# Attention and feed-forward kernel on one core: conversions merged four slots after their first operation instead of three, raw loads a slot later, the second group normalised on ScalarE

## The chip, the cores and the metric

The kernel runs on one core of a Trainium2 chip. The time is device microseconds of one execution; several runs are taken and their median is compared. PE is TensorE (matmuls; PEld its weight loads), DVE is VectorE, ACT is ScalarE, POOL is GpSimd, SP is SyncE, which here issues all DMAs.

## What is computed

Causal attention over 4 batches, 12 heads, 448 positions and a head size of 64, then RMS normalisation and a gated feed-forward layer on all 1792 rows:

```python
attn = softmax(where(causal, q @ k.T / 8, -1e9))      # per batch and head
x    = concat_heads(attn @ v)                          # 1792 x 768
xn   = x / sqrt(mean(x * x) + 1e-6) * rms_g
g    = xn @ w_gate                                     # 768 x 1536
out  = (silu(g) * (xn @ w_val)) @ w_out                # back to 768
```

The three weight matrices come as 64-bit floats and are turned into 32-bit floats on the core. Each feed-forward product is formed from split operands (a high part and the remainder), so that it takes three matmuls.

## The kernel before

**Groups.** Attention is cut into 60 units, each one pair of heads of one batch (or two batches for the last short pieces) and a range of queries. Units 0 to 11 are the first group, 12 to 23 the second, 24 to 59 the third. While the attention of a group runs, the feed-forward part of the group before it runs between its pieces: the feed-forward of group 1 (512 rows) beside the attention of group 2, and so on. The third group's feed-forward comes at the end with no attention beside it.

**Slots.** The order of all instructions is written out by a loop on the host. It counts slots (`tick`, L137): in each slot it issues six feed-forward matmuls (`ffn_part`, L426, two of the six chunks of a weight unit, so three slots make a unit of 18 matmuls), then perhaps one step of attention, and then whatever was posted for this slot. `post(n, f)` (L131) puts `f` n slots later. The numbers n are in the table `T` (L44). Each engine executes its instructions in the order of issue, so a slot later means behind other instructions in that engine's queue.

**Weight units.** There are 36 units of weights (gate and value chunks alternate, then the output matrix). For each:

- `load_w` (L357) loads the raw 64-bit words into one of three buffers (tag `w64`), in the DMA queue of SP.
- `convert_ops` (L368) has five operations with slots c0, c1, c2, c3, c5: ACT scales the high word into the new tile `w_c` (L379); POOL clears the high words that are not wanted (L380), which waits for ACT's operation; DVE merges low and high words (L382), which waits for POOL's, and then merges them into `w_c` (L384); SP stores `w_c` to DRAM (L386) for later. L384 is the last reader of the raw buffer.
- `split_w` (L389) casts `w_c` to the high part `w_h` on ACT (L394), and DVE or POOL forms the remainder `w_l` (L396 on DVE in this stretch).

The conversion of unit s+5 begins, the split of unit s+3 is posted, in the last slot of unit s; the load of unit s+7 is posted at the beginning of unit s, `ld` slots later.

**Evictions.** A unit's 18 matmuls fill one of two PSUM banks `m`. `evict` (L446) empties it on DVE: for a gate unit into `gr` (L457), followed by a tanh on ACT (L458) and a product (L459); for a value unit into `t_sb` (L467), followed by the cast `hh` (L468, ACT) and the remainder `hl` (L470, DVE). PE can begin unit s only when unit s-2 has been evicted, since it takes the same bank.

**Attention of a unit.** Scores on PE (L192), the masked, scaled copy with its minimum on DVE (L201), the exponential on ACT (L204, and L227 for the sums), the reciprocal on DVE (L213), the normalising of the four pieces (`norms`; L207 on ACT or L209 on POOL), transposes on PE (L249), copies of these out of PSUM (L253 DVE, L255 ACT), and the products with v (L275, PE). Which engine normalises is decided in `softmax` (L195): before, ACT has it for units 15 to 23, POOL for all others. `norm` (L212) runs seven slots after the scores in this group.

Of the kernel before, what the change touches and what calls it, by code (L numbers as in the profile page):

```python
# [38 lines left out]
        for g in range(NG) for c in range(NP)}  # L39
ENDS = [max(i for i, u in enumerate(UNITS) if u[0] == g) + 1 for g in range(NG)]  # L40
MASKED = -8.0e9


T = dict(c0=0, c1=1, c2=3, c20=12, c3=3, c30=13, c26=6, c36=7, c5=5, c50=16, c56=9, exp=1, exp0=3, gt=1, hh=1, hl=4, ws=5, ld2=7,  # L44
         ld=3, ld1=11, lv=5, norm0=7, norm1=2, r0=1, r1=5, so=3, wl=2, wl0=7, wl2=5, wl4=0, xl=2, xl0=9)
LOAD = (4, 12, 24, 36, 48, 60, 74, 86)
CONVERT = (20, 32, 44, 56, 62, 93)
SPLIT = (33, 45, 57, 70)
# [14 lines left out]
def attention_ffn(ctx: ExitStack, tc: tile.TileContext, qk0, qk1, qk2, v, v2, w, g, out, out2):  # L63
# [30 lines left out]
    def bank(tag, bufs=1):  # L94


        return ps.tile([P, W], F32, tag=tag, name=tag + "_ps", bufs=bufs)

    def f32(ap):
        return ap.bitcast(F32)  # L100
# [30 lines left out]
    def post(delay, fn):  # L131
        if delay <= 0:
            fn()
        else:
            later.setdefault(now[0] + delay, []).append(fn)
# [7 lines left out]
    xr, xh, xl, acc, xq = {}, {}, {}, {}, {}  # L143
# [6 lines left out]
    def load_qk(p):  # L150
        if p < len(UNITS):
            _, kind, _, _, row, _ = UNITS[p]
            raw_qk[p] = raw.tile([P, 2, W], F32, tag="qk", name="qk_r")
            if kind == 2:
                nc.sync.dma_start(out=raw_qk[p], in_=qk2[row])
            else:
                nc.sync.dma_start(out=raw_qk[p][:, 0], in_=(qk0, qk1)[kind][row])
# [10 lines left out]
    def blocks(kind):  # L168

        return [(0, P), (P, 2 * P)] if kind == 0 else [(0, KEYS[kind])]  # L170

    def steps_s(p):


        if not 0 <= p < len(UNITS):
            return []
        _, kind, _, _, _, _ = UNITS[p]
        pr = hs[p] = dict(norms=[])
        bl = blocks(kind)
        nb = 2 * len(bl)  # L180

        def scores(pss):
            for i, (o, wd) in enumerate(bl):
                for h in range(1 + (kind == 2)):
                    for e in range(2):
                        r = raw_qk[p][e * D: (e + 1) * D, h]
                        if kind == 2:
                            ps, q0, nq = pss[e][h * D: (h + 1) * D, :wd], 0, D
                        else:
                            ps, q0, nq = pss[e][:, o: o + wd], i * P, P  # L190
                        k0 = nq if kind else 2 * P
                        nc.tensor.matmul(ps, r[:, q0: q0 + nq], r[:, k0: k0 + wd],  # L192
                                         start=True, stop=True)

        def softmax(e, i, pss):  # L195
            o, wd = bl[i]
            ps, sp = pss[e][:, o: o + wd], pr["sp"][e][:, o: o + wd]
            n = len(bl) * e + i
            nm, sm, rs = (pr[m][:, n: n + 1] for m in ("nm", "sm", "rs"))
            mk = mask2 if kind == 2 else mask[:, 3 * P - wd:]  # L200
            nc.vector.tensor_tensor_reduce(  # L201
                out=sp, in0=ps, in1=mk, scale=nsc, scalar=3.0e38,
                op0=ALU.add, op1=ALU.min, accum_out=nm)
            post(T["exp" if p >= ENDS[0] else "exp0"], lambda: nc.scalar.activation(  # L204
                sp, sp, AF.Exp, bias=nm, scale=-1.0, accum_out=sm))
            if ENDS[0] + 3 <= p < ENDS[1]:
                pr["norms"].append(lambda: nc.scalar.mul(sp, sp, rs))  # L207
            else:
                pr["norms"].append(lambda: nc.gpsimd.tensor_scalar(  # L209
                    sp, sp, rs, 1.0, op0=ALU.mult, op1=ALU.mult))  # L210

        def norm():  # L212
            nc.vector.reciprocal(pr["rs"][:, :nb], pr["sm"][:, :nb])  # L213
            for f in pr["norms"]:
                f()

        def step():
            for nm in ("nm", "sm", "rs"):
                pr[nm] = st_p.tile([P, 4], F32, tag=nm, name=nm)
            pr["sp"] = [sp_p.tile([P, S], F32, tag="sp", name="sp") for _ in range(2)]  # L220
            pss = [bank(t_) for t_ in "xy"] if p > ENDS[1] + DP and p % 2 == 0 else [
                bank("s", 2) for _ in range(2)]
            scores(pss)
            for e in range(2):
                for i in range(len(bl)):
                    softmax(e, i, pss)
            post(T["exp" if p >= ENDS[0] else "exp0"], lambda: nc.scalar.activation(  # L227
                pr["sm"][:, :nb], pr["sm"][:, :nb], AF.Identity, bias=tiny))
            post(T["norm1" if kind else "norm0"], norm)
            post(2, lambda: load_qk(p + 4))  # L230

        return [step]
# [64 lines left out]
    def square(b, c):  # L297
# [19 lines left out]
        if c == NP - 1:  # L317
            post(T["r1" if b else "r0"], lambda: rms(b, [acc[b, 0]] if b else [acc[b, 0], sq]))
        waiting.append((b, c))

    def split_x():
        if not waiting:
# [5 lines left out]
        nc.scalar.mul(h, x, gc)  # L328
        post(T["xl0" if b == 0 and c < NP - 1 else "xl"], lambda: nc.vector.scalar_tensor_tensor(
            out=l, in0=x, scalar=gc, in1=f32(h), op0=ALU.mult, op1=ALU.subtract))  # L330
        xh[b, c], xl[b, c] = h, l

    def rms(b, parts):

        ps = bank("t")
        for i, sq in enumerate(parts):
            nc.tensor.matmul(ps, ones, sq, start=(i == 0), stop=(i == len(parts) - 1))
        r = rinv[b] = rm_p.tile([P, W], F32, tag="rms", name="rms", bufs=2)
        nc.scalar.activation(r, ps, AF.Sqrt, bias=eps, scale=1.0 / DM)
        for i in range(W // P):  # L340
            sl = slice(i * P, (i + 1) * P)
            post(i if b else 1, lambda sl=sl: nc.vector.reciprocal(r[:, sl], r[:, sl]))
# [25 lines left out]
    def convert_ops(s):  # L368
# [6 lines left out]
        hf_ = raw_w.bitcast(F32)[:, :, 1]  # L375
        at2, at3, at5 = [T[n] for n in ("c20 c30 c50" if s < 5 else "c26 c36 c56" if s == 5 else "c2 c3 c5").split()]

# [427 lines left out]
    with tc.manual_schedule():  # L805
# [157 lines left out]
        for q in range(21):  # L963
            i, p = divmod(q, 3)
# [58 lines left out]
```

## Time and profile before

| | us |
|---|---|
| median of three runs | 699.96 (698.40 to 701.52) |
| the profiled execution | 699.28 |
| its span, first to last instruction | 697.5 |
| PE busy in the span | 672.7 |
| DVE, ACT, POOL busy | 534.1, 371.7, 321.5 |

The conversions run from the beginning to about 240 us. The change bears on those from unit 6 on, that is on the stretch from about 70 us on. Engine busy shares are of the whole span; PE's idle time is what the span can lose as long as PE's work stays the same. PEclk in a view is TensorE's granted clock, 1.00 being 2.4 GHz and 0.50 being 1.2 GHz.

### The profile page before, as it was taken

What the parts mean: (1) busy time and instruction counts of PE and PEld (TensorE: products, weight loads), DVE (VectorE), ACT (ScalarE), POOL (GpSimd) and SP (SyncE); (2) the same over time, 40 slices, a digit from 0 to 9 for tenths busy, and PEclk for the clock granted to TensorE, in tenths of its full rate; (3) what the DMA queues carried; (4) which work ended last, traced back from release to release, by engine and by line L of the source; (5) the groups of instructions that cost most, each with busy time, mean ns of one, the idle gap of its engine ahead of it and who ended that gap; (6) DMA issues with size and microseconds to landing.
All of it is one profiled execution on the core that took longest, in us unless ns stands there. A gap on an engine that the chain in (4) does not pass through costs nothing. (4 is left out here: it accounts for less than half of the span.)

```text
span 697.5 us, 11924 instructions
## 1 busy us (share of the span) xinstructions
PE 672.7 (96%) x4108; PEld 551.0 (79%) x4108; DVE 534.1 (77%) x1048; ACT 371.7 (53%) x832; POOL 321.5 (46%) x293
## 2 busy tenths in 40 slices
PE   9889799999999999999999999999999999999997
PEld 6456676677677777777778676888999999999997
DVE  4996988778887867677777878479386768679993
ACT  6974556876868544544545455444433433355550
POOL 4993263121223536567485756754354536312220
PEclk9999999999999999999999999999999999999999
DMA  8663878687769647667667674334657576552541
GB/s 268 225 223 108 250 220 264 201 279 209 241 203 343 219 139 207 208 223 242 203 206 229 197 237 156 123 121 133 200 184 247 180 246 207 206 159 81 168 139 68
DMA packets 71356, 138.80 MB, mean 199 GB/s; under 512 B 7744, under 2 KB 39232, under 8 KB 71296
## 3 DMA queue, kind: packets, MB, share of 16 engines
q1 hardware_dynamic: 71296, 138.05, 61.3%
q8 instruction: 32, 0.52, 0.3%
q14 instruction: 28, 0.23, 0.1%
HBM read 104.21 MB, written 33.82 MB: 198 GB/s over the span
## 5 line engine op out<-in xcount | busy, mean ns | idle before, releaser
L209 POOL TENSOR_SCALAR sp<-sp,rs 128x384 f32<-128x384 f32 (+3 forms) x132 | 95.8, 743 | 90.5 <-DVE rs L213 79.8
L440 PE MATMUL m_ps<-xh,w_h 128*128 128x512 f32 x276 | 119.0, 431 | 5.6 <-DVE gr L457 3.7
L204 ACT ACTIVATE sp<-sp,nm 128x384 f32<-128x384 f32 (+3 forms) x168 | 87.2, 522 | 43.5 <-DVE nm L201 43.5
L442 PE MATMUL m_ps<-xh,w_l 128*128 128x512 f32 x276 | 109.5, 397 | 0.0
L441 PE MATMUL m_ps<-xl,w_h 128*128 128x512 f32 x276 | 109.4, 396 | 0.0
L380 POOL TENSOR_SCALAR w<-w 128x768 f32<-128x768 f32 x36 | 36.6, 1017 | 98.1 <-ACT w_c L379 78.4
L103 POOL TENSOR_TENSOR a_l<-w_q,a_h 128x768 fp32r<-128x768 f32 x24 | 47.3, 1969 | 66.6 <-ACT a_h L481 66.5
L275 PEld LDWEIGHTS a_ps<-pt,v_r 128*64 128x64 f32 (+1 forms) x864 | 42.2, 137 | 37.5 <-DVE pt L253 10.4
L275 PE MATMUL a_ps<-pt,v_r 128*64 128x128 f32 (+2 forms) x864 | 60.8, 268 | 9.6 <-DVE pt L253 5.8
L440 PEld LDWEIGHTS m_ps<-xh,w_h 128*128 128x128 f32 x276 | 52.6, 191 | 19.2 <-issue 8.1
L103 POOL TENSOR_TENSOR w_l<-w_r,w_h 128x768 fp32r<-128x768 f32 x30 | 59.6, 1993 | 7.0 <-ACT w_h L394 6.9
L442 PEld LDWEIGHTS m_ps<-xh,w_l 128*128 128x128 f32 x276 | 52.5, 190 | 12.0
L253 DVE COPY pt<-t_ps 128x384 f32<-128x384 f32 (+1 forms) x71 | 42.5, 598 | 23.7 <-PE t_ps L249 23.3
L441 PEld LDWEIGHTS m_ps<-xl,w_h 128*128 128x128 f32 x276 | 52.9, 192 | 8.1 <-issue 0.2
L440 PE MATMUL m_ps<-hh,w_h 128*128 128x512 f32 x144 | 58.6, 407 | 0.0
L201 DVE CUSTOM_DVE_ANT_0 sp<-s_ps,mask 128x128 f32<-128x128 f32 (+3 forms) x136 | 49.8, 415 | 9.6 <-PE s_ps L192 8.6
L441 PE MATMUL m_ps<-hl,w_h 128*128 128x512 f32 x144 | 56.3, 391 | 0.7 <-DVE hl L470 0.7
L442 PE MATMUL m_ps<-hh,w_l 128*128 128x512 f32 x144 | 56.3, 391 | 0.0
L249 PE MATMUL t_ps<-ident,sp 128*128 128x128 f32 (+1 forms) x309 | 50.3, 275 | 0.4 <-POOL sp L209 0.2
L249 PEld LDWEIGHTS t_ps<-ident,sp 128*128 128x128 f32 (+1 forms) x309 | 38.0, 138 | 14.9 <-POOL sp L209 2.2
L382 DVE SCALAR_TENSOR_TENSOR w<-w 128x768 int32<-128x768 int32 x36 | 36.2, 1006 | 14.4 <-POOL w L380 14.4
L192 PE MATMUL s_ps<-qk_r 64*128 64x128 f32 (+3 forms) x296 | 42.2, 420 | 0.5 <-DVE nm L201 0.4
(185 smaller groups left out, 1671.1 us busy)
## 6 DMA issues: line engine op xcount, KB each, us to landing
w<-in_w SPq DMA_DIRECT2D x36, 768.0 KB, 5.1
w<-w_c SPq DMA_DIRECT2D x36, 384.0 KB, 5.7
w_r<-w SPq DMA_DIRECT2D x36, 384.0 KB, 4.9
qk_r<-in_qk SPq DMA_DIRECT2D x48, 256.0 KB, 4.4
qk_r<-in_qk SPq DMA_DIRECT2D x12, 512.0 KB, 5.6
v_r<-in_v SPq DMA_DIRECT2D x12, 448.0 KB, 5.2
v_r<-in_v SPq DMA_DIRECT2D x24, 192.0 KB, 3.0
wy<-w_r SPq DMA_DIRECT2D x24, 192.0 KB, 4.0
```

Source lines behind the costliest of these rows:

```text
L103: nc.gpsimd.tensor_tensor(out_, a, b, op=op)
L192: nc.tensor.matmul(ps, r[:, q0: q0 + nq], r[:, k0: k0 + wd], start=True, stop=True)
L201: nc.vector.tensor_tensor_reduce(out=sp, in0=ps, in1=mk, scale=nsc, scalar=3.0e38, op0=ALU.add, op1=ALU.min, accum_out=nm)
L204: post(T["exp" if p >= ENDS[0] else "exp0"], lambda: nc.scalar.activation(sp, sp, AF.Exp, bias=nm, scale=-1.0, accum_out=sm))
L209: pr["norms"].append(lambda: nc.gpsimd.tensor_scalar(sp, sp, rs, 1.0, op0=ALU.mult, op1=ALU.mult))
L249: nc.tensor.transpose(ps[:kb, at: at + P], pr["sp"][e][:, o + kb * j: o + kb * (j + 1)], ident)
L253: nc.vector.tensor_copy(pt[:kb, :at], ps[:kb, :at])
L275: nc.tensor.matmul(av_ps[e * D: (e + 1) * D, p % 2, q0: q0 + n], raw_v[p][:kb, h, j, e, :], pr["pt", e][:kb, a0: a0 + n], start=(j == 0), ...
L380: (T["c1"], lambda: nc.gpsimd.tensor_scalar(hf_, hf_, 0.0, 1.0, op0=ALU.mult, op1=ALU.mult)),
L440: nc.tensor.matmul(ps, wh[:, k, :], mh, start=(first and k == ks[0]), stop=False)
L441: nc.tensor.matmul(ps, wh[:, k, :], ml, start=False, stop=False)
L442: nc.tensor.matmul(ps, wl[:, k, :], mh, start=False, stop=(last and k == 5))
```

## The change

```diff
@@ -41,8 +41,8 @@
 MASKED = -8.0e9
 
 
-T = dict(c0=0, c1=1, c2=3, c20=12, c3=3, c30=13, c26=6, c36=7, c5=5, c50=16, c56=9, exp=1, exp0=3, gt=1, hh=1, hl=4, ws=5, ld2=7,
-         ld=3, ld1=11, lv=5, norm0=7, norm1=2, r0=1, r1=5, so=3, wl=2, wl0=7, wl2=5, wl4=0, xl=2, xl0=9)
+T = dict(c0=0, c1=1, c2=4, c20=12, c3=4, c30=13, c26=6, c36=7, c5=6, c50=16, c56=9, exp=1, exp0=3, gt=1, hh=1, hl=4, ws=5, ld2=7,
+         ld=4, ld1=11, lv=5, norm0=7, norm1=2, r0=1, r1=5, so=3, wl=2, wl0=7, wl2=5, wl4=0, xl=2, xl0=9)
 LOAD = (4, 12, 24, 36, 48, 60, 74, 86)
 CONVERT = (20, 32, 44, 56, 62, 93)
 SPLIT = (33, 45, 57, 70)
@@ -203,7 +203,7 @@
                 op0=ALU.add, op1=ALU.min, accum_out=nm)
             post(T["exp" if p >= ENDS[0] else "exp0"], lambda: nc.scalar.activation(
                 sp, sp, AF.Exp, bias=nm, scale=-1.0, accum_out=sm))
-            if ENDS[0] + 3 <= p < ENDS[1]:
+            if ENDS[0] <= p < ENDS[1]:
                 pr["norms"].append(lambda: nc.scalar.mul(sp, sp, rs))
             else:
                 pr["norms"].append(lambda: nc.gpsimd.tensor_scalar(
```

Four entries of the table and one condition are changed. Units are counted from 0. For conversions of unit 6 and later, the two merges on DVE (L382, L384) are posted four slots after the conversion's first operation, not three; the store of the converted unit (L386) six, not five; the raw load (L360) of unit 8 and later four slots after the beginning of the unit that issues it, not three. The condition in `softmax` now gives ACT the normalising of units 12 to 14 too, 12 instructions that POOL had. The number and order of PE's instructions stay as they are; DVE keeps its number of instructions.

The first place is DVE's queue around the eviction of unit 4 (`gr` from `m_ps`), for which PE waits before unit 6. (In names, `w64` is a raw buffer, `w_c` a converted unit, and the last number tells one tile from another.) Before:

```order
L384 SCALAR_TENSOR_TENSOR w_c_981<-w_c_981,w64_911 128x768
L459 SCALAR_TENSOR_TENSOR t_sb_1010<-t_sb_1010,gr_1009 128x512
L467 TENSOR_TENSOR t_sb_1010<-t_sb_1010,x_ps_986 128x512
L396 TENSOR_TENSOR w_l_1040<-w_c_961,w_h_1039 128x768
L382 SCALAR_TENSOR_TENSOR w64_964<-w64_964 128x768
L384 SCALAR_TENSOR_TENSOR w_c_1042<-w_c_1042,w64_964 128x768
L457 TENSOR_TENSOR gr_1071<-m_ps_1048,rms_924 128x512
L470 TENSOR_TENSOR hl_1037<-t_sb_1010,hh_1036 128x512
L459 SCALAR_TENSOR_TENSOR t_sb_1072<-t_sb_1072,gr_1071 128x512
L201 ISA sp_1095,nm_1092<-s_ps_1097,mask_104 128x128
```

And now:

```order
L459 SCALAR_TENSOR_TENSOR t_sb_1009<-t_sb_1009,gr_1008 128x512
L467 TENSOR_TENSOR t_sb_1009<-t_sb_1009,x_ps_984 128x512
L382 SCALAR_TENSOR_TENSOR w64_911<-w64_911 128x768
L384 SCALAR_TENSOR_TENSOR w_c_979<-w_c_979,w64_911 128x768
L396 TENSOR_TENSOR w_l_1038<-w_c_961,w_h_1037 128x768
L457 TENSOR_TENSOR gr_1069<-m_ps_1046,rms_924 128x512
L470 TENSOR_TENSOR hl_1035<-t_sb_1009,hh_1034 128x512
L382 SCALAR_TENSOR_TENSOR w64_968<-w64_968 128x768
L384 SCALAR_TENSOR_TENSOR w_c_1040<-w_c_1040,w64_968 128x768
L459 SCALAR_TENSOR_TENSOR t_sb_1070<-t_sb_1070,gr_1069 128x512
```

The pair L382, L384 stood ahead of the eviction `gr` and stands behind it and behind L470 now; the pair ahead of L396 is the one of the conversion before, which has moved in the same way, behind L467.

The second place is ACT's queue a little later, behind the first operation of a conversion (L379), where the exponentials of the next unit (L204) follow. Before:

```order
L394 CAST w_h_1075<-w_c_981 128x768
L379 ACTIVATE w_c_1078<-w64_983 128x768
L204 ACTIVATE sp_1095,sm_1093<-sp_1095,nm_1092 128x128
L204 ACTIVATE sp_1095,sm_1093<-sp_1095,nm_1092 128x256
L204 ACTIVATE sp_1096,sm_1093<-sp_1096,nm_1092 128x128
L204 ACTIVATE sp_1096,sm_1093<-sp_1096,nm_1092 128x256
L227 ACTIVATE sm_1093<-sm_1093,tiny_121 128x4
```

And now:

```order
L394 CAST w_h_1073<-w_c_979 128x768
L379 ACTIVATE w_c_1076<-w64_1006 128x768
L207 ACTIVATE sp_994<-sp_994,rs_993 128x128
L207 ACTIVATE sp_994<-sp_994,rs_993 128x256
L207 ACTIVATE sp_995<-sp_995,rs_993 128x128
L207 ACTIVATE sp_995<-sp_995,rs_993 128x256
L204 ACTIVATE sp_1093,sm_1091<-sp_1093,nm_1090 128x128
L204 ACTIVATE sp_1093,sm_1091<-sp_1093,nm_1090 128x256
L204 ACTIVATE sp_1094,sm_1091<-sp_1094,nm_1090 128x128
```

Four normalising operations of unit 12 stand between L379 and the exponentials. The same happens for units 13 and 14. They were POOL's before (L209), between two of its L380.

The third place is DVE's queue around the eviction of a value unit later in the stretch, where PE waits for `t_sb`. Before:

```order
L459 SCALAR_TENSOR_TENSOR t_sb_1987<-t_sb_1987,gr_1986 128x512
L396 TENSOR_TENSOR w_l_1997<-w_c_1878,w_h_1996 128x768
L382 SCALAR_TENSOR_TENSOR w64_1881<-w64_1881 128x768
L384 SCALAR_TENSOR_TENSOR w_c_1999<-w_c_1999,w64_1881 128x768
L467 TENSOR_TENSOR t_sb_1987<-t_sb_1987,m_ps_2006 128x512
```

And now:

```order
L459 SCALAR_TENSOR_TENSOR t_sb_1985<-t_sb_1985,gr_1984 128x512
L396 TENSOR_TENSOR w_l_1995<-w_c_1876,w_h_1994 128x768
L467 TENSOR_TENSOR t_sb_1985<-t_sb_1985,m_ps_2004 128x512
L382 SCALAR_TENSOR_TENSOR w64_1890<-w64_1890 128x768
L384 SCALAR_TENSOR_TENSOR w_c_1997<-w_c_1997,w64_1890 128x768
```

The eviction L467 has moved ahead of the pair of merges. SP's queue keeps its instructions; a raw load (L360) moves behind a load of queries and keys (L157) in some units, and ahead of none.

## Rows read from the trace of the kernel before

**Rows 1.** The page, busy time of each engine (share of the span, instructions).

```profile
PE 672.7 (96%) x4108; PEld 551.0 (79%) x4108; DVE 534.1 (77%) x1048; ACT 371.7 (53%) x832; POOL 321.5 (46%) x293
```

**Rows 2.** Timeline of PE: start us, duration us, operation, [idle before <-releaser].

```profile
84.44 0.76 PE L440 MATMUL m_ps<-xh,w_h 128*128 128x512 f32 x1 [3.72 <-DVE gr L457]
...
102.29 0.47 PE L440 MATMUL m_ps<-xh,w_h 128*128 128x512 f32 x1 [0.68 <-DVE t_sb L467]
...
107.96 0.86 PE L275 MATMUL a_ps<-pt,v_r 128*64 128x256 f32 x6 [1.26 <-ACT pt L255]
...
133.11 0.86 PE L275 MATMUL a_ps<-pt,v_r 128*64 128x256 f32 x6 [1.53 <-ACT pt L255]
...
183.03 0.50 PE L440 MATMUL m_ps<-xh,w_h 128*128 128x512 f32 x1 [1.20 <-DVE t_sb L467]
...
198.79 0.50 PE L441 MATMUL m_ps<-hl,w_h 128*128 128x512 f32 x1 [0.66 <-DVE hl L470]
```

**Rows 3.** Timeline of DVE, 79 to 91 us.

```profile
79.98 0.95 DVE L396 TENSOR_TENSOR w_l<-w_c,w_h 128x768 fp32r<-128x768 f32 x1
...
81.69 0.96 DVE L382 SCALAR_TENSOR_TENSOR w<-w 128x768 int32<-128x768 int32 x1 [0.76 <-POOL w L380]
...
82.74 0.96 DVE L384 SCALAR_TENSOR_TENSOR w_c<-w_c,w 128x768 int32<-128x768 int32 x1
...
83.61 0.68 DVE L457 TENSOR_TENSOR gr<-m_ps,rms 128x512 f32<-128x512 f32 x1
...
86.80 1.53 DVE L396 TENSOR_TENSOR w_l<-w_c,w_h 128x768 fp32r<-128x768 f32 x1
...
90.17 0.68 DVE L467 TENSOR_TENSOR t_sb<-t_sb,m_ps 128x512 f32<-128x512 f32 x1
```

**Rows 4.** Timeline of POOL, 80 to 82 us.

```profile
80.57 1.08 POOL L380 TENSOR_SCALAR w<-w 128x768 f32<-128x768 f32 x1 [6.94 <-ACT w_c L379]
```

**Rows 5.** Windows: stretch, length; busy PE, PEld, DVE, ACT, POOL; PEclk, DMA share, GB/s.

```profile
45.00:50.00 5.00, 3.36 (x20) 2.28 (x20) 4.84 (x8) 4.17 (x13) 4.92 (x5) 1.00 0.36 131
...
80.00:85.00 5.00, 1.28 (x5) 0.76 (x4) 4.05 (x7) 1.61 (x4) 1.08 (x1) 0.87 0.73 242
...
85.00:90.00 5.00, 5.00 (x13) 3.92 (x12) 4.91 (x13) 4.97 (x13) 3.36 (x3) 0.50 0.82 272
```

**Rows 6.** Timeline of PE, two matmuls of one unit, three apart.

```profile
73.81 0.39 PE L442 MATMUL m_ps<-xh,w_l 128*128 128x512 f32 x1
...
74.49 0.39 PE L442 MATMUL m_ps<-xh,w_l 128*128 128x512 f32 x1
```

**Rows 7.** Timeline of DVE and ACT, 127 to 133 us.

```profile
127.89 0.96 DVE L382 SCALAR_TENSOR_TENSOR w<-w 128x768 int32<-128x768 int32 x1 [0.89 <-POOL w L380]
...
129.82 0.68 DVE L457 TENSOR_TENSOR gr<-m_ps,rms 128x512 f32<-128x512 f32 x1
...
132.60 0.46 ACT L255 COPY pt<-x_ps 128x384 f32<-128x384 f32 x1
```

**Rows 8.** Timeline of DVE, 179 to 196 us.

```profile
179.85 0.96 DVE L382 SCALAR_TENSOR_TENSOR w<-w 128x768 int32<-128x768 int32 x1 [0.84 <-POOL w L380]
...
182.31 0.68 DVE L467 TENSOR_TENSOR t_sb<-t_sb,m_ps 128x512 f32<-128x512 f32 x1
...
195.49 0.93 DVE L382 SCALAR_TENSOR_TENSOR w<-w 128x768 int32<-128x768 int32 x1
```

**Rows 9.** Timeline of POOL and ACT: normalising one unit of the second group.

```profile
87.50 4.59 POOL L209 TENSOR_SCALAR sp<-sp,rs 128x128 f32<-128x128 f32 x4
...
121.70 1.50 ACT L207 ACTIVATE sp<-sp,rs 128x128 f32<-128x128 f32 x4 [1.15 <-DVE rs L213]
```

**Rows 10.** Raw loads, 60 to 260 us: one issue, its first reader, time to landing of all.

```profile
210.83 0.33 SPq L360 DMA_DIRECT2D w<-in_w  x1
...
218.56 0.91 ACT L379 ACTIVATE w_c<-w 128x768 f32<-128x768 f32 x1
...
DMA to landing us min/median/max: 4.7/5.1/7.0
```

## The prediction

> **What bounds the kernel.** I read the page's busy times first: PE is busy 672.7 of the 697.5 us of the span [rows 1], so PE sets the time, and its work and order are the same after the change. The time can only move by what PE idles (24.8 us in all) and by its clock. Next I read PE's waits stretch by stretch, and then its timeline at each long one. In the stretch that the change touches (from 70 us until the conversions end near 240 us) there are six waits over half a microsecond: 3.72, 0.68, 1.26, 1.53, 1.20 and 0.66 us, together 9.05 [rows 2]. Four of them name a DVE operation that empties a bank or forms an operand, two name ACT's copy of transposes. Then I read DVE's and POOL's timelines to see what DVE was doing while PE waited, and the windows for the clock.
>
> At the first wait DVE finished L396 at 80.93, had nothing to do for 0.76 us because its next instruction, the merge L382, waits for POOL's clearing [rows 3], which itself came only behind ACT's scaling [rows 4], then did the two merges, and only then, at 83.61, the eviction `gr` for which PE had waited since 80.7. The bank could have been emptied at once: its matmuls had ended one unit earlier. While PE stood, its clock fell: the mean is 0.87 in 80 to 85 us, and 0.50 (1.2 GHz) in 85 to 90 us, right behind the wait [rows 5]. So this place costs far more than 3.72 us.
>
> **The change part by part.** The profiled execution took 699.28 us, of which 697.5 are the span; 699.28 is the base of the sum, 0.68 below the median of the runs (699.96).
>
> *A, the wait at 84.44.* The eviction is now directly behind that L396. It starts near 80.93 and not 83.61, so PE's wait shrinks by 2.7 to about 1.0 us. Nothing ahead of it becomes later: the pair of merges that moved in from the conversion before takes the place of itself, since L459 and L467 went ahead of it. **-2.7.**
>
> *B, the clock.* The trace does not show what a wait of 1.0 us does there; it is bounded by the row with 3.72 us of waiting, which was followed by half the clock, and by the window 45 to 50, where PE idled 1.64 of 5 us and the clock stayed 1.00 [rows 5]. 1.0 is on the side of the second, so I take the full clock. From 84.44 to 90.00 at half rate PE did 5.56 us of work that takes 2.78 at the full rate. **-2.8**, with 0 as the other end.
>
> *C, the next unit's bank.* Before unit 7, PE needs the eviction L467 of unit 5. DVE's instructions between `gr` and that L467 are the same set before and after, only in another order. From start to start they took 6.56 us [rows 3]. Of this, 0.58 was that L396 took 1.53 us beside POOL and not 0.95 as the one at 79.98; POOL's clearing is done earlier now, so I take 5.98. L467 then starts at 86.9 and PE can go on at 87.6. PE's unit 6 begins at 81.7 and is 18 matmuls, three of which take 0.68 us at full clock [rows 6], so 4.1 us: it is done at 85.8. A new wait of 1.8 us, which the half clock hid before (PE was then so slow that DVE caught up). **+1.8**; by 6.56 it is 2.4, and if PE's restart or DVE's queue gain a little, 0.6.
>
> *D, the wait at 102.29.* L467 of unit 7 goes ahead of its pair of merges, but all of DVE is at its limit here, and I expect 0.35 of the 0.68 to stay. **-0.3.**
>
> *E, the normalising.* For units 12 to 14 POOL loses three times 4.59 us and ACT gets three times 1.50 [rows 9]. On POOL the next clearing L380 stood behind the normalising; it is now done at once. On ACT the exponentials, the cast L394 and the scaling L379 are queued behind it, and all of them behind its wait for the reciprocal, 4.5 us in all. That lengthens ACT's queue ahead of the copies at 107.96. Against it, `gr`, and so the tanh in front of the second copy, no longer stands behind a merge that waits for POOL. I take these as equal, so that the copy comes earlier by what PE has won by then and PE waits its 1.26 us as before. **0**, between +1.5 (a round's normalising) and -1.26 (the wait goes).
>
> *F, the wait at 133.11.* ACT's copy came at 132.60, behind a tanh that waited for `gr` at 129.82, which DVE did behind a merge that had waited 0.89 for POOL [rows 7]. The eviction now stands ahead of that pair. **-1.5.**
>
> *G, the waits at 183.03 and 198.79.* L467 at 182.31 came behind the merge at 179.85 that had waited 0.84 for POOL, and its partner; it is ahead of them now, some 2.5 us earlier, more than PE's 1.20. At 198.79 the operand `hl` stood behind the merges at 195.49 [rows 8] and is now ahead of them, more than the 0.66 earlier. **-1.9.**
>
> *H, what is late next.* The merges, L459, the scores' copies L201 and the reciprocal come a little later relative to PE, and PE comes earlier by six. Somewhere an eviction or a copy will be late in its place. The trace can't show where; between 0 and 1.5 (the longest wait of this kind left in rows 2), I take 0.6, near the 0.68 of an ordinary late eviction. **+0.6.**
>
> *The store and the raw load.* L386 a slot later delays nothing that PE reads in this stretch, since the copy in DRAM is read in the next round of weights. The raw load starts when L384 frees its buffer. The shortest time between an issue and its first reader is 7.73 us, and loads land in 5.1 us, at most 7.0 [rows 10]. The merge moves behind one eviction and its followers, 0.6 to 2.6 us by rows 3, so the shortest becomes 5.1 to 7.1: at the edge in the worst, covered in the usual case. Nothing, with a rival below for the edge.
>
> Sum: 699.28 - 2.7 - 2.8 + 1.8 - 0.3 + 0 - 1.5 - 1.9 + 0.6 = 692.5 us. Behind the conversions PE's order is unchanged, and PE is the busy engine [rows 1], so I let what is won arrive whole at the end.
>
> **A rule against B.** The row shows the clock at 1.00 in a window where PE idled a third of the time in pieces [rows 5]. The Trainium skill, "TensorE: Matmul & The Clock Gate", section "A second HAM failure mode: psum-queue depth-cycling", says that small gaps of PE between groups of matmuls that cycle through PSUM banks can be frequent enough that the clock swings between its two levels. By that rule the waits of A and C, both for a bank, would still halve the clock here and the time would be that of rival 1. The windows of this kernel speak for the other.
>
> **The rivals.**
>
> 1. *The clock falls all the same.* Two waits, 1.0 and 1.8 us, with 4.1 us of work between them, in a stretch that lost the clock before. Against it: 45 to 50 us. B is then 0, and C mostly hidden again by the slow PE: 692.5 + 2.8 - 1.2 = 694.1 at best, 695.3 with C whole. Chance 0.12.
> 2. *ACT is late and takes the later gains back.* E costs its 1.5, and F and G come back as waits for ACT's copies, whose queue is longer: 692.5 + 1.5 + 1.7 (half of F and G) = 695.7. For it: two of the six waits name ACT's copy. Against it: ACT is busy 53%. Chance 0.12.
> 3. *The wait only moves one unit on.* DVE is the limit from 66 to 100 us; if C is 2.4, the clock falls there and H is 1.5, then A and B come back whole and only F and G stay: 699.28 - 3.4 + 1.5 = 697.4. Chance 0.11.
> 4. *Raw loads come late: slower.* The mechanism is the raw load's issue behind L384, and its place is ACT's L379, which waits for the data with the copies and casts queued behind it. It decides once the time from issue to reader is below the landing: 7.0 against 5.1 to 7.1. If every second of 28 loads is late by 0.9 (7.0 less 6.1, the middle) and all reaches PE, 12.6 us: 692.5 + 12.6 = 705. Against it: the usual landing is 5.1. Chance 0.04.
>
> That the change does not do what it says is excluded for its moves: the queues of DVE, ACT and POOL show the pairs behind the evictions and the normalising on ACT.
>
> **How the numbers follow.** The forecast, 692.5, has the chance left, 0.61; its own range is 689.8 to 695 (C at 0.6 and no H at the one end, less a part of the wait at 107.96; E or C at their worse ends at the other). Low: 689.5. High: 697.0, which takes in rivals 1 and 2 and the 0.7 us by which the median can lie above the profiled execution; left out are rivals 3 and 4 and a rest of the forecast. A measurement of this kernel can tell about 0.5% from no change, 3.5 us, so faster means below 696.5: the forecast, rival 1 and most of rival 2 give 0.83. Rival 3 and the rest of rival 2 give 0.13 for the same, rival 4 gives 0.04 for slower.
>
> **What would show it.** PE's wait of 3.72 us for `gr` is about 1 us, no window behind it has PEclk 0.50, and a new wait of one to two microseconds for `t_sb` (L467) stands 5 to 6 us later; L382's waits for POOL on DVE shrink; PE's waits at 133, 183 and 199 us are gone. L207 has 12 pieces more and L209 12 fewer. It is wrong if PEclk still falls near 85 us, if ACT's L379 waits for a DMA, or if the time behind the conversions changes.

## The result, and the profile after

| | before | after |
|---|---|---|
| median of 4 runs each, us | 700.44 (698.40 to 701.52) | 692.62 (691.53 to 692.95) |
| span of the profiled execution, us | 697.5 | 689.8 |

The ratio is 0.9889, with a 95% interval from 0.9863 to 0.9915: the change is 1.1% faster. The forecast was 692.5 us, in a range from 689.5 to 697.0. The total came out; the experiments show that some of the terms it was summed from did not.

The page of the kernel after, busy time of each engine, against [rows 1]:

```profile
PE 669.2 (97%) x4108; PEld 548.8 (80%) x4108; DVE 537.5 (78%) x1048; ACT 375.2 (54%) x844; POOL 312.3 (45%) x281
```

PE's busy time fell by 3.5 us, most of it by the clock behind the first wait (term B of the prediction estimates 2.8 us there), and its idle time by 4.2. Its timeline after shows the waits that stand where those of [rows 2] stood (start us, duration us, operation, idle before and releaser); they are all those over 0.25 us between 60 and 240 us:

```profile
81.87 0.47 PE L440 MATMUL m_ps<-xh,w_h 128*128 128x512 f32 x1 [1.05 <-DVE gr L457]
...
88.32 0.47 PE L440 MATMUL m_ps<-xh,w_h 128*128 128x512 f32 x1 [2.08 <-DVE t_sb L467]
...
99.39 0.47 PE L440 MATMUL m_ps<-xh,w_h 128*128 128x512 f32 x1 [0.88 <-DVE t_sb L467]
...
103.90 0.65 PE L275 MATMUL a_ps<-pt,v_r 128*64 128x256 f32 x2 [0.69 <-ACT pt L255]
104.82 0.86 PE L275 MATMUL a_ps<-pt,v_r 128*64 128x256 f32 x6 [0.28 <-ACT pt L255]
```

The 3.72 us for `gr` are 1.05, the new wait for L467 before unit 7 is 2.08, and the waits at 133, 183 and 199 us are gone. The windows of the kernel after, with the columns of [rows 5]:

```profile
80.00:85.00 5.00, 3.95 (x18) 2.96 (x17) 4.97 (x7) 3.18 (x5) 2.14 (x2) 1.00 0.79 206
85.00:90.00 5.00, 2.92 (x14) 1.89 (x14) 4.91 (x14) 3.24 (x12) 0.00 (x1) 1.00 1.00 320
```

The granted clock is 1.00 in both; before, it was 0.87 and 0.50. DVE's timeline after, beside [rows 3]:

```profile
80.17 0.95 DVE L396 TENSOR_TENSOR w_l<-w_c,w_h 128x768 fp32r<-128x768 f32 x1
81.04 0.69 DVE L457 TENSOR_TENSOR gr<-m_ps,rms 128x512 f32<-128x512 f32 x1
...
82.33 0.95 DVE L382 SCALAR_TENSOR_TENSOR w<-w 128x768 int32<-128x768 int32 x1
...
84.18 1.35 DVE L459 SCALAR_TENSOR_TENSOR t_sb<-t_sb,gr 128x512 f32<-128x512 f32 x1
...
86.65 0.92 DVE L396 TENSOR_TENSOR w_l<-w_c,w_h 128x768 fp32r<-128x768 f32 x1
87.50 0.67 DVE L467 TENSOR_TENSOR t_sb<-t_sb,m_ps 128x512 f32<-128x512 f32 x1
...
91.10 0.96 DVE L396 TENSOR_TENSOR w_l<-w_c,w_h 128x768 fp32r<-128x768 f32 x1 [1.01 <-ACT w_h L394]
```

`gr` starts at 81.04 and not 83.61, directly behind L396, and the merge L382 no longer stands idle. Two things differ from the forecast. L459 took 1.35 us, not the 0.69 it takes in e12 (an experiment below, without POOL's clearing): it ran from 84.18 beside POOL's clearing, which began at 84.08. And the L396 at 91.10 stood 1.01 us for ACT's cast, which no row of before had at this place.

How much of DVE's standing went over the whole stretch is seen in its groups by line, 60 to 250 us (form and count, busy us and mean ns, idle before us and releaser), first before, then after:

```profile
L396 DVE TENSOR_TENSOR w_l<-w_c,w_h 128x768 fp32r<-128x768 f32 x32 | 33.0, 1031 | 3.1 <-ACT w_h L394 3.0
L384 DVE SCALAR_TENSOR_TENSOR w_c<-w_c,w 128x768 int32<-128x768 int32 x31 | 32.4, 1044 | 2.6
L382 DVE SCALAR_TENSOR_TENSOR w<-w 128x768 int32<-128x768 int32 x31 | 30.3, 976 | 14.4 <-POOL w L380 14.4
...
L459 DVE SCALAR_TENSOR_TENSOR t_sb<-t_sb,gr 128x512 f32<-128x512 f32 x12 | 9.3, 774 | 3.2 <-ACT t_sb L458 2.4
```

```profile
L396 DVE TENSOR_TENSOR w_l<-w_c,w_h 128x768 fp32r<-128x768 f32 x32 | 36.3, 1135 | 4.3 <-ACT w_h L394 4.3
L384 DVE SCALAR_TENSOR_TENSOR w_c<-w_c,w 128x768 int32<-128x768 int32 x31 | 33.8, 1089 | 1.8
L382 DVE SCALAR_TENSOR_TENSOR w<-w 128x768 int32<-128x768 int32 x31 | 29.9, 963 | 0.8 <-POOL w L380 0.8
L459 DVE SCALAR_TENSOR_TENSOR t_sb<-t_sb,gr 128x512 f32<-128x512 f32 x12 | 10.2, 854 | 0.9 <-ACT t_sb L458 0.8
```

DVE stood 14.4 us for POOL's clearing before and stands 0.8 now: 13.6 us are freed. Part is spent again: L396, L384 and L459 take 5.6 us more in sum for the same number of instructions, and L396 stands 1.3 us longer for ACT.

**Where the time came from.** I take the first score matmul (L192) of each round (the turn of one attention unit) as a mark and subtract its start before from its start in the other kernel. The first row lies ahead of the places that differ most: what stands in it, 0.00 to 0.78 us, is the offset of that one execution, and a gain counted from the first mark has it taken off. The last row is behind the conversions; some rounds are left out.

| mark before, us | after | e1 | e2 | e4 | e6 | e10 | e12 |
|---|---|---|---|---|---|---|---|
| 67.60 | 0.10 | 0.11 | 0.44 | 0.31 | 0.78 | 0.09 | 0.00 |
| 92.96 | -3.10 | -3.07 | 0.11 | -2.89 | 0.34 | -3.11 | -2.83 |
| 105.21 | -2.92 | -3.66 | 0.64 | 0.20 | -0.57 | -3.83 | -3.74 |
| 117.87 | -3.09 | -4.98 | 0.76 | 0.31 | -2.46 | -5.01 | -5.57 |
| 130.07 | -3.16 | -5.04 | 1.45 | 0.99 | -2.53 | -5.08 | -5.64 |
| 143.02 | -4.53 | -6.01 | 1.46 | 2.95 | -4.36 | -6.37 | -7.52 |
| 178.52 | -4.99 | -6.47 | 1.45 | 2.49 | -4.82 | -6.83 | -7.98 |
| 190.83 | -6.53 | -8.01 | 1.45 | 1.53 | -6.35 | -8.36 | -9.52 |
| 203.91 | -7.47 | -8.95 | 1.43 | 1.56 | -7.30 | -9.31 | -10.47 |
| 226.56 | -7.70 | -9.44 | 1.43 | 1.52 | -7.58 | -9.70 | -11.56 |
| 298.15 | -7.72 | -9.45 | 1.44 | 1.55 | -7.57 | -9.67 | -11.53 |

In the kernel after, 3.2 us are won before 93 us (from +0.10 to -3.10), nothing between 93 and 130, 1.4 before 143, 0.5 before 179, 1.5 and 0.9 in the two rounds behind, and 0.2 more. Everything is won by 227 us and arrives whole. The other columns belong to the experiments, which follow.

### The profile page after: what moved, and what is told of

It is laid out like the page before. It is cut to its first block, busy times and chain, and to the rows that moved or that the text cites. A ratio compares the mean times of both kernels' runs of the same rounds, so it can differ in the third digit from the quotient of the medians.

```text
span 689.8 us, 11922 instructions
## 1 busy us (share of the span) xinstructions
PE 669.2 (97%) x4108; PEld 548.8 (80%) x4108; DVE 537.5 (78%) x1048; ACT 375.2 (54%) x844; POOL 312.3 (45%) x281
## 5 line engine op out<-in xcount | busy, mean ns | idle before, releaser
L209 POOL TENSOR_SCALAR sp<-sp,rs 128x128 f32<-128x128 f32 (+2 forms) x120 | 82.2, 704 | 89.5 <-DVE rs L213 84.7
L440 PE MATMUL m_ps<-xh,w_h 128*128 128x512 f32 x276 | 117.6, 426 | 4.0 <-DVE t_sb L467 3.0
L204 ACT ACTIVATE sp<-sp,nm 128x384 f32<-128x384 f32 (+3 forms) x168 | 87.1, 521 | 39.7 <-DVE nm L201 39.7
L380 POOL TENSOR_SCALAR w<-w 128x768 f32<-128x768 f32 x36 | 40.1, 1113 | 101.6 <-ACT w_c L379 93.5
L103 POOL TENSOR_TENSOR a_l<-w_q,a_h 128x768 fp32r<-128x768 f32 x24 | 47.1, 1964 | 66.6 <-ACT a_h L481 66.5
L103 POOL TENSOR_TENSOR w_l<-w_r,w_h 128x768 fp32r<-128x768 f32 x30 | 59.5, 1990 | 7.3 <-ACT w_h L394 7.1
L396 DVE TENSOR_TENSOR w_l<-w_c,w_h 128x768 fp32r<-128x768 f32 x36 | 40.1, 1114 | 4.3 <-ACT w_h L394 4.3
L384 DVE SCALAR_TENSOR_TENSOR w_c<-w_c,w 128x768 int32<-128x768 int32 x36 | 41.5, 1153 | 2.0
```

The costliest lines, as they stand in the source:

```text
L103: nc.gpsimd.tensor_tensor(out_, a, b, op=op)
L209: pr["norms"].append(lambda: nc.gpsimd.tensor_scalar(sp, sp, rs, 1.0, op0=ALU.mult, op1=ALU.mult))
L384: (at3, lambda: nc.vector.scalar_tensor_tensor(out=ti, in0=ti, scalar=3, in1=lo, op0=ALU.logical_shift_left, op1=ALU.bitwise_or)),
L440: nc.tensor.matmul(ps, wh[:, k, :], mh, start=(first and k == ks[0]), stop=False)
```

## Experiments

Two theories stood at the start. By the first, DVE's queue is the limit in the whole stretch: what counts is how long it stands for POOL, and PE's waits and its clock are only where that shows. By the second, the first place (the wait of 3.72 us and the half clock behind it) carries most of the gain. Where an expectation numbers its theories, the text behind it says in words which one held. Medians of before in the three sets of runs were 700.58 (e1 to e4), 699.85 (e5 to e8) and 699.98 us (e9 to e12). Each run has 4 to 10 executions, e5 and e9 only two; the marks come from one execution each.

| run | what it is | median us | ratio to before, 95% interval |
|---|---|---|---|
| e1 | slots alone | 690.53 | 0.9849 [0.9834, 0.9864] |
| e2 | normalising alone | 701.55 | 1.0014 [0.9996, 1.0033] |
| e3 | PE kept busy in the wait | 700.95 | 1.0003 [0.9989, 1.0017] |
| e4 | change, slots only for units 6 to 9 | 701.85 | 1.0012 [0.9998, 1.0026] |
| e5 | change, old slots for store and raw load | 691.82 | 0.9883 [0.9850, 0.9915] |
| e6 | slots alone, only from unit 10 | 691.77 | 0.9882 [0.9862, 0.9902] |
| e7 | slots alone, one more | 693.10 | 0.9903 [0.9882, 0.9923] |
| e8 | e1, rest of unit 7 on POOL | 693.78 | 0.9907 [0.9878, 0.9936] |
| e9 | change, raw load two slots later | 691.43 | 0.9874 [0.9842, 0.9907] |
| e10 | change, normalising one slot later | 690.21 | 0.9858 [0.9835, 0.9881] |
| e11 | e8, but ahead in POOL's queue | 691.32 | 0.9878 [0.9855, 0.9900] |
| e12 | before without the clearing from unit 6 | 687.76 | 0.9823 [0.9803, 0.9844] |

### e1 and e2: the two halves apart

The slots without the normalising (against the change):

```diff
-            if ENDS[0] <= p < ENDS[1]:
+            if ENDS[0] + 3 <= p < ENDS[1]:
```

> The slots alone (merges at four, store at six, raw load at four), with POOL normalising units 12 to 14 as before. Theory 1 (the evictions moved ahead of the merges carry the gain): nearly all of it stays, 692.5 to 693.8 us, first wait for gr about 1 us, PEclk 1.00 in 85 to 90 us. Theory 2 (the normalising taken off POOL carries a good part, since POOL's clearing stood behind it): 695 us or more.

The normalising without the slots (against before):

```diff
-            if ENDS[0] + 3 <= p < ENDS[1]:
+            if ENDS[0] <= p < ENDS[1]:
```

> The normalising of units 12 to 14 on ACT alone, the slots as before. Theory 1: the first wait of 3.7 us and the half clock behind it stay, since they come before the first of these pieces; only the merges' waits for POOL of 1.2 us near 93 and 104 us go; 698 to 700 us. Theory 2: 697 us or less.

The slots alone give 690.53 us: the first theory held, with more gain than it expected, and more than the whole change has. In the table of marks e1 equals the change up to 93 us, is ahead by 1.9 at 118 (-4.98 against -3.09), and by 1.7 at the end. The normalising alone costs 1.0 us by its marks (from 0.44 to 1.44), which the runs' interval can't tell from nothing; 701.55 us lies above the 698 to 700 us that I expected. PE's timeline of e1 has three waits in this stretch, and none near 99 or 104 us:

```profile
81.90 0.47 PE L440 MATMUL m_ps<-xh,w_h 128*128 128x512 f32 x1 [1.06 <-DVE gr L457]
...
88.34 0.47 PE L440 MATMUL m_ps<-xh,w_h 128*128 128x512 f32 x1 [2.08 <-DVE t_sb L467]
...
127.10 0.86 PE L275 MATMUL a_ps<-pt,v_r 128*64 128x256 f32 x6 [0.57 <-ACT pt L255]
```

So the late eviction at 99.39 and the two late copies at 103.90 and 104.82 in the change come from the normalising, whose cost I had set equal to a gain of the slots without pricing either.

### e10: what the normalising costs

Against the change, the four operations of units 12 to 14 are posted one slot behind the reciprocal that they read:

```diff
-                f()
+                post(1 if ENDS[0] <= p < ENDS[0] + 3 else 0, f)
```

> The change, with the normalising of units 12 to 14 on ACT one slot behind the reciprocal instead of in its slot, so that the exponentials stand ahead of it in ACT's queue. Theory 1 (what the normalising costs is ACT standing 2.8 us before each of these groups for DVE's reciprocal, with exponentials and casts queued behind): most of the 1.7 us comes back, 690.5 to 691.3 us. Theory 2 (it costs by its work on ACT, 4.5 us in all, wherever it stands): 692 to 693 us.

690.21 us, a little below the 690.5 to 691.3 us of the first theory: the cost is gone, and the marks equal e1's within 0.4 us throughout. ACT's timeline in the change, then in e10:

```profile
86.76 1.49 ACT L207 ACTIVATE sp<-sp,rs 128x128 f32<-128x128 f32 x4 [2.83 <-DVE rs L213]
88.16 0.39 ACT L204 ACTIVATE sp<-sp,nm 128x128 f32<-128x128 f32 x1
...
90.25 0.82 ACT L394 CAST w_h<-w_c 128x768 fp32r<-128x768 f32 x1
```

```profile
85.83 0.40 ACT L204 ACTIVATE sp<-sp,nm 128x128 f32<-128x128 f32 x1 [1.91 <-DVE nm L201]
...
87.93 1.48 ACT L207 ACTIVATE sp<-sp,rs 128x128 f32<-128x128 f32 x4
89.31 0.82 ACT L394 CAST w_h<-w_c 128x768 fp32r<-128x768 f32 x1
```

In the change, ACT stands 2.83 us for the reciprocal (L213), with the exponentials and the cast L394 behind it in the queue, though both could have run; the cast ends late and DVE's L396 stands for it (the 1.01 at 91.10 above, and the same again at 102.18). In e10 the exponentials go first and the cast starts 0.94 us sooner. That ACT does the work costs nothing; that it waits for its operand at the head of its queue costs 1.7 to 1.9 us. e1 and e10 can't be told apart (0.9849 and 0.9858). That both are ahead of the change rests on the marks: at the last one, counted from the first, e1 and e10 stand at -9.56 and -9.76, the change and its variants e5 and e9 at -7.82, -7.86 and -7.98. The intervals of the three ratios touch or overlap.

### e3: the clock by itself

Before's kernel, with 14 small matmuls of ones into a spare bank ahead of unit 6 (their result is not used):

```diff
+                if s == 6 and k0 == 0:
+                    fill = bank("y")
+                    for _ in range(14):
+                        nc.tensor.matmul(fill[:, :P], ones, ones, start=True, stop=True)
```

> The kernel before with 14 small matmuls (128 columns, into an idle bank, results unused) ahead of unit 6, in the place where PE waits 3.7 us. PE's work comes no earlier, but PE stands still for only some 0.5 us. Theory 1 (clock and DVE are one bound here): the clock stays at 1.00, unit 6 takes 4.1 us, and unit 7 then waits about 2.4 us for the eviction L467, which DVE can't give earlier; the scores that stood at 92.96 us come at 92.0 to 92.6, and the time is 698.4 to 699.5. Theory 2 (the half clock costs its 2.8 us by itself, terms B and C of the prediction are separate): those scores come near 90.2 and the time is about 696.5.

The window of e3 behind the first wait, and PE's waits in its timeline:

```profile
85.00:90.00 5.00, 3.77 (x17) 2.80 (x15) 4.91 (x13) 4.97 (x13) 3.35 (x3) 1.00 0.82 278
```

```profile
84.45 0.47 PE L440 MATMUL m_ps<-xh,w_h 128*128 128x512 f32 x1 [0.58 <-DVE gr L457]
...
91.00 0.47 PE L440 MATMUL m_ps<-xh,w_h 128*128 128x512 f32 x1 [2.23 <-DVE t_sb L467]
...
102.30 0.47 PE L440 MATMUL m_ps<-xh,w_h 128*128 128x512 f32 x1 [1.08 <-DVE t_sb L467]
```

The clock stayed at 1.00 where it had fallen to 0.50, and the time did not move: ratio 1.0003, marks equal to before's from 105 us on. PE did its work faster and then stood 2.23 us for `t_sb` at 91.00, where before had no wait, and 1.08 at 102.30 instead of 0.68. PE at half clock had cost nothing, because DVE came no sooner. The first theory held, without the few tenths of gain that it gave.

### e4 and e6: the first place against the rest

The new slots for units 6 to 9 only (e4, with the change's normalising), or from unit 10 on only (e6, with before's). d2, d3 and d5 are the old slots, and the raw load is cut in the same way:

```diff
-        at2, at3, at5 = [T[n] for n in (... else "c2 c3 c5").split()]
+        at2, at3, at5 = [T[n] for n in (... else "c2 c3 c5" if s < 10 else "d2 d3 d5").split()]
```

(e6 has `s >= 10` there.)

> The change, but with the later slots for conversions of units 6 to 9 only; from unit 10 on the slots are as before. Theory 1 (the gain comes in steps at each place where an eviction stood behind a waiting merge): the first step of about 3.1 us stays, the steps near 133, 183 and 199 us are gone: 695.3 to 697 us. Theory 2 (the first wait and the clock behind it are the gain): 692.5 to 693.5 us.

> The later slots for conversions of unit 10 and up only, units 6 to 9 as before, POOL normalising as before. Theory 1 (until about 105 us DVE is the bound and its waits for POOL's clearing, not PE's wait, are the loss; the early slots alone gained nothing at the end): the first wait of 3.7 us and the half clock are there, yet most of the 9.4 us of the slots alone comes in steps behind 92 us: 692 to 695 us. Theory 2 (each place is worth its own wait): the 3.1 us of the first place are missing in full, and the time is 693.5 to 694 at the least, with the steps behind it as in the run of the slots alone.

e4 missed what I expected of it. It wins the same 3.2 us as the change by 93 us and has given all of it back by 105. At the end it stands at +1.24 from its first mark, against +1.00 for e2, which has the normalising without any slots: the early slots won nothing that lasted. PE's waits of over 1.5 us in e4 behind 90 us:

```profile
95.90 0.47 PE L440 MATMUL m_ps<-xh,w_h 128*128 128x512 f32 x1 [1.96 <-DVE gr L457]
...
102.48 0.47 PE L440 MATMUL m_ps<-xh,w_h 128*128 128x512 f32 x1 [1.53 <-DVE t_sb L467]
...
134.47 0.86 PE L275 MATMUL a_ps<-pt,v_r 128*64 128x256 f32 x6 [1.91 <-ACT pt L255]
```

From unit 10 on DVE still has the old order and stands 13.5 us for POOL in the stretch (before 14.4), so PE comes earlier and waits longer, 1.96 us for the next `gr` among others. e6 is the mirror: the wait of 3.70 us remains, with half the clock behind it (0.66 in 85 to 90 us), and yet the end is won: 691.77 us, just below the first theory's 692 to 695. PE's two waits over 0.25 us in e6 between 60 and 240 us, and DVE's waits for POOL in its view of waits (us, times, longest):

```profile
85.21 0.62 PE L440 MATMUL m_ps<-xh,w_h 128*128 128x512 f32 x1 [3.70 <-DVE gr L457]
...
91.76 0.47 PE L440 MATMUL m_ps<-xh,w_h 128*128 128x512 f32 x1 [0.61 <-DVE t_sb L467]
```

```profile
DVE w L382 <- POOL w L380: 1.8, 6, 0.8
```

Counted from the first mark, e6 wins 8.35 us and e1 9.56. The first place, the largest wait in this stretch with 3.2 us at its own mark, is worth 1.2 at the end (with the other early units), and nothing without the rest. The second theory falls.

### e12: all of the standing

Before's kernel without POOL's clearing L380 from unit 6 on, so that those weights are left unconverted; the order is otherwise before's.

```diff
-        return [
+        return [o for o in [
...
-        ]
+        ] if s < 6 or o[0] != T["c1"]]
```

> The kernel before without POOL's clearing of the high words (L380) for units 6 and up, which leaves the weights of these units unconverted; the order of all else is the same. So the merges no longer wait for POOL, but evictions still stand behind them. Theory 1 (the loss is DVE standing for POOL, 14.4 us in 15 waits): the first wait is about 3 us (0.76 less), the waits at 108, 133 and 183 us shrink by what the merge had waited, 693 to 696 us. Theory 2 (the merges' own 1.9 us ahead of each eviction are the loss): 698 us or more. Theory 3 (the standing is all of it): 691.5 us or less.

687.76 us and -11.53 at the marks. That is more than the first theory's 693 to 696 us and in the range of the third, by which the standing is all of the loss. The evictions stand behind the merges here as they did before; the only wait of PE over 0.25 us between 60 and 239 us is:

```profile
82.62 0.47 PE L440 MATMUL m_ps<-xh,w_h 128*128 128x512 f32 x1 [1.90 <-DVE gr L457]
```

So DVE's standing for POOL, and not the place of the evictions as such, is where the loss lies: an eviction behind a pair of merges costs little by itself (the one wait left), but much behind a merge that stands for POOL. e12 removes two things at once, the standing and POOL's work beside DVE (its L396 is down to 952 ns in the mean, from 1031), and does not tell them apart. Nor does any run move the evictions ahead and leave the standing as it was, so what the new order is worth by itself is not shown.

### e7: one slot more

```diff
-T = dict(... c2=4, ... c3=4, ... c5=6, ... ld=4, ...)
+T = dict(... c2=5, ... c3=5, ... c5=7, ... ld=5, ...)
```

> The slots alone, once more a slot later: merges at five, store at seven, raw load at five, POOL normalising as before. Theory 1 (what counts is that evictions stand ahead of merges that still wait; at four the merges hardly wait, 0.8 us in all): nothing more to be had, 690 to 691.5 us. Theory 2 (each slot gives room): 688.5 us or less. Rival: the split's cast stands right behind the merge and the loads come later, so that ACT waits: 692 us or more.

693.1 us, 2.6 behind e1: with 0.8 us of standing left there was nothing more to free, and the rival came out, for the reason that it gave for the cast (no wait of ACT for a load shows). ACT's waits for the merge ahead of the cast L394, 60 to 250 us, in e1 and then in e7 (us, times, longest):

```profile
ACT w_h L394 <- DVE w_c L384: 0.9, 1, 0.9
```

```profile
ACT w_h L394 <- DVE w_c L384: 6.5, 7, 1.6
```

PE stands 1.05 us for ACT's copy at 210.09 that was not late in e1. Its first two waits are close to e1's (1.06 and 2.08), but the clock is not, as the windows show:

```profile
81.41 0.47 PE L440 MATMUL m_ps<-xh,w_h 128*128 128x512 f32 x1 [0.64 <-DVE gr L457]
...
87.94 0.47 PE L440 MATMUL m_ps<-xh,w_h 128*128 128x512 f32 x1 [2.17 <-DVE t_sb L467]
```

```profile
85.00:90.00 5.00, 2.83 (x14) 1.80 (x14) 4.88 (x7) 2.66 (x6) 5.00 (x5) 0.94 0.58 165
90.00:95.00 5.00, 5.00 (x22) 3.65 (x21) 4.90 (x14) 3.01 (x8) 1.26 (x2) 0.72 0.98 375
```

Counted from the first mark, e7 is 0.9 us behind e1 at the mark of 105.21, later than these windows, and 1.0 at that of 190.83; 2.0 more are lost by that of 226.56, with a granted clock of 1.00 in every window from 180 to 225 us. So at most 0.9 us can be the clock's, and how much of it is, was not tried.

### e5 and e9: the store and the raw load

e5 is the change with `c5=5` and `ld=3`, e9 the change with `ld=6`.

> The change with the store and the raw load left at their old slots (five and three): only the merges and the normalising moved. The raw load waits for L384 in SP's queue either way. Theory 1 (store and load were moved only to keep the queue in step): as the change, 691.5 to 693.5 us. Theory 2 (the load's slot matters, through what stands behind it in SP's queue): over 694 us.

> The change with the raw load two slots later still (six). Theory 1 (the load has room of a few microseconds, and ACT's waits for it are caught up before PE sees them): ACT's L379 waits for loads some us in all instead of once 1.1 us, the time 692 to 695 us. Theory 2 (the prediction's rival 4: every late load reaches PE): 700 us or more.

691.82 and 691.43 us, both within the error of the change (e9 a little better than its first theory), whose marks e5 follows to 0.04 us at the end (-7.86 and -7.82 from the first mark). The shortest time from a load's issue to its reader is 5.70 us in the change, 5.72 in e5 and 5.23 in e9; ACT's L379 stands once for a load in each, 1.14, 0.79 and 0.59 us, and no wait of PE follows. The store's and the load's slots are worth nothing either way.

### e8 and e11: the new wait before unit 7

In e1 DVE's L396 of unit 7 stands ahead of L467, for which PE waits 2.08 us. e8 gives that one operation to POOL in its turn; e11 gives it to POOL too, but issues it at once behind its cast, ahead of the normalising. The edit of e8 against e1:

```diff
-            if s < NU or s > NU + 2 * NF and s % 2:
+            if s < NU and s != 7 or s > NU + 2 * NF and s % 2:
```

> The slots alone, and the remainder w_l of unit 7 on POOL in place of DVE (one instruction of 0.92 us ahead of the eviction for which PE waits 2.08 us). Theory 1 (DVE's work up to that eviction is what PE waits for): the wait becomes about 1.2 us and the time 689.6 to 689.9 us. Rival (DVE's next instruction waits for something else, or POOL's remainder is late for PE): the wait stays near 2 us, 690.4 us or more.

> The slots alone, with the remainder w_l of unit 7 on POOL as in the run before, but issued at once behind its cast, ahead of POOL's normalising. Theory 1: the wait of 2.08 us is about 1.2 us, no wait for w_l, 689.5 to 690 us. Rival (beside POOL's two microseconds DVE's own instructions become slower, as L459 with 1.35 us did beside a clearing): 690.4 us or more.

e8's wait for L467 fell to 1.24 as expected, but the operation came late on POOL, and PE stood for it. PE's timeline of e8, then POOL's:

```profile
93.27 0.80 PE L442 MATMUL m_ps<-xh,w_l 128*128 128x512 f32 x1 [4.95 <-POOL w_l L103]
```

```profile
87.07 3.90 POOL L209 TENSOR_SCALAR sp<-sp,rs 128x128 f32<-128x128 f32 x4 [1.91 <-DVE rs L213]
90.94 2.28 POOL L103 TENSOR_TENSOR w_l<-w_c,w_h 128x768 fp32r<-128x768 f32 x1
```

The 4.95 us come of its place behind 3.90 us of normalising and of its own 2.28 us on POOL: the rival, by its second reason. In e11 it goes first, and now DVE is slower. POOL's timeline of e11, then DVE's:

```profile
83.28 1.85 POOL L103 TENSOR_TENSOR w_l<-w_c,w_h 128x768 fp32r<-128x768 f32 x1 [1.34 <-ACT w_h L394]
85.09 1.57 POOL L380 TENSOR_SCALAR w<-w 128x768 f32<-128x768 f32 x1
```

```profile
83.38 2.56 DVE L384 SCALAR_TENSOR_TENSOR w_c<-w_c,w 128x768 int32<-128x768 int32 x1
85.86 1.34 DVE L459 SCALAR_TENSOR_TENSOR t_sb<-t_sb,gr 128x512 f32<-128x512 f32 x1
```

L384 took 2.56 us and not 0.96; L459, 1.34, was as slow in the change and in e1 (1.35). So DVE lost 1.60 us on L384 for the 0.92 that it gave away, and PE's wait grew from 2.08 to 2.83. The rival held: what DVE gave to POOL came back as a slower DVE operation. Neither beats e1.

## Why the prediction was right, and where not

- **The mechanism: held; what bounds: only in part.** DVE's evictions stood behind merges that stood for POOL. With the pairs behind the evictions the standing went from 14.4 to 0.8 us, and e12 shows the standing, together with POOL's work beside DVE, to be worth more than all that the change wins. But I took PE as the bound throughout. Up to about 105 us DVE's queue is the bound: e3 gave PE its clock back there, and nothing came of it.
- **A, B and C (-2.7, -2.8, +1.8): right at their place, wrongly founded.** Forecast -3.7, measured -3.2 at the mark behind unit 6. The wait of 1.05 and the full clock came as said; the new wait was 2.08, since DVE took 6.46 us from `gr` to L467 (81.04 to 87.50), within my two ends of 5.98 and 6.56. But I let this arrive whole because PE is the busy engine. e4 shows it given back within one round, e3 that B alone gives nothing, e6 that the place is worth 1.2 at the end. It stayed in the change because later places were freed too.
- **D (-0.3): no.** The wait became 0.88, not 0.35. In e1 it is gone, so it is the normalising's doing.
- **E (0): near in its net, wrong in both halves.** Between the marks at 92.96 and 130.07 the change wins 0.06 us, where D and E together gave 0.3. In e1 the waits of 0.68 and 1.26 are both gone and these marks win 1.97: the slots alone give what I had as E's better end, and all of D. The normalising takes 1.9 of it back there (1.7 at the end; 1.0 alone, in e2), beyond the +1.5 that I had as E's worse end. I listed what is queued behind ACT's wait for the reciprocal and then set the two effects equal without pricing the cast, for which DVE stands; that they came out nearly equal is luck. This is rival 2's cause at about its price; F and G, which that rival took back, did come.
- **F and G (-1.5, -1.9): held, G too small by 0.6.** The marks give -1.4 before 143 us and, for G's two places, -1.5 and -0.9. Not forecast were 0.5 us before 179 and 0.2 before 227 us; [rows 2] have no wait there. At the second place before's trace has one of 0.48 us (a copy, at 216.65), below the half microsecond from which I read them.
- **H (+0.6): not seen** apart from what E brought: behind 105 us PE has no wait over 0.25 us in this stretch.
- **The rivals.** The clock stayed (1); the wait did move one unit on, but with the clock at 1.00 the gain behind it stayed (3). Rival 4's sign, one of the three that I had named for being wrong, appeared: ACT's L379 stood once for a load, 1.1 us. No wait of PE came behind it, and e9 with the load two slots later still loses nothing, so the sign was a poor one. The shortest time from issue to reader, 5.70 us, is within the 5.1 to 7.1 I gave.

So 692.5 was right by parts that erred both ways. The marks of the change give -7.8 us and not the -6.8 of the sum: A to C won 0.5 less and D to F some 0.4 less, G won 0.6 more, 0.7 came where nothing was forecast, and H's 0.6 did not come. By causes, the slots win 9.6 us and the normalising takes 1.7. That the median, 692.62, lies 0.1 from the forecast is partly luck: the base of the sum, 699.28, was 1.2 below the median of before as measured here, 700.44, and that made up for the 1.0 us too little.

## What to carry to other kernels

In this kernel an engine with a queue in order, DVE, limited a stretch. In such a case count what that queue stands for over the whole stretch, and not the waits of the engine behind it: the largest wait of PE in the stretch, 3.7 us, was worth 1.2. An instruction that waits for a third engine belongs behind those that others wait for, and work that moves to another engine belongs a slot behind its operand there, or what is queued behind it pays. Before a gain at one place is carried to the end, look whether the same standing waits at the next.

## What the runs showed of the hardware

- **The clock after short waits.** With waits of PE of 1.05 and 2.08 us it stayed at 1.00 though PE was busy only 2.92 of 5 us (the change, 85 to 90 us). With 0.64 and 2.17 it fell to 0.94 and 0.72 (e7), and with one of 1.90 to 0.87 and 0.79 (e12, 80 to 90 us). With 1.05 and 2.83 it stayed at 1.00 (e11, 80 to 95 us). So the length of these waits does not order the cases. The Trainium skill, "TensorE: Matmul & The Clock Gate", section "A second HAM failure mode: psum-queue depth-cycling", says of a kernel in bf16 that small gaps between groups that cycle through banks made the clock swing; the change's trace, at 1.00, does not agree; e7's, at 0.72, is in line with it. What decides between the cases stays open.
- **DVE beside POOL.** In e11 POOL's L103 ran from 83.28 for 1.85 us and DVE's L384, begun 0.10 later, ended at 85.94, 0.81 us behind POOL's end (85.13) and so near its own 0.96 behind it. POOL's L380, begun at 85.09, took 1.57 us and ended 0.72 behind that L384; ahead of DVE's instruction it took 0.89 (before, at 86.64). The Trainium skill, "SBUF — State Buffer", section "Who interferes with whom", says that a DVE instruction with two SBUF inputs contends with a GpSimd one that reads SBUF, that the pair of ports which they share is an exclusive lock, and that the order of issue decides who blocks; the rows agree, within 0.2 us. Such a collision, L459's 1.35 at 84.18, is part of the 5.6 us that the three lines of DVE took more in the change; how much of it is of this kind was not counted.
